# Loading the last 128 rows of w4 apart, onto the DMA engines with the lowest numbers

## Chip, cores and metric

One core of one Trainium2 chip. The metric is device time in microseconds (us) of one execution, median of several; lower is better. The span in a profile runs from the first to the last instruction and is some 1.8 us shorter than the device time.

## The reference, cut to what matters

```python
xn = _layernorm(A_x)                               # (4, 1, 576)
out = x + A(xn, k_cache, v_cache, wq, wo) + B(xn, w1, w2, w3, w4)
# A: one query per batch, 32 heads on 16 K/V heads, the last 2048 keys, times wo
# B: x1 = xn + hs (with one position the shifted branch is zero)
h2 = _gelu(_layernorm(x1) @ w3) @ w4               # w4: (4608, 576)
```

Nearly all of the work is reading: 16 K and 16 V tiles of 2 MB, wq, wo, w3, and w4 last.

## The kernel before

All loads but the 4.5 KB of x go from SyncE in one order: K and V by heads, wo by quarters, w3 after the third V, w4 at the very end, in six pieces. w4 is seen as 36 slots of 128 rows; slot u is one product per half of the output.

```python
W4_PIECES = [0, NFH, NF - 12, NF - 6, NF - 2, NF - 1, NF]      # NF = 36, NFH = 18

def load_w4():
    t = wp.tile([P, NF, D], BF16, tag="w", name="w4_sb")
    for lo, hi in zip(W4_PIECES, W4_PIECES[1:]):
        e = lo // NFH
        src = B_w4[e * (F // 2):(e + 1) * (F // 2), :].rearrange("(p i) n -> p i n", i=NFH)
        nc.sync.dma_start(out=t[:, lo:hi, :], in_=src[:, lo - e * NFH:hi - e * NFH, :])
# ... the end of the kernel:
    o_pick(hl)
    o_proj(hl)
    for lo, hi in pieces:
        mlp_out(lo, hi)          # gT[:, u, :] times w4[:, u, :], u from lo to hi
    # cast to bf16 on VectorE and ScalarE, one output DMA from SyncE
```

## Time and profile before

| | before |
|---|---|
| device time | 211.46 us (211.37 to 211.50, 3 runs) |
| span of the profiled run | 209.7 us |
| DMA: bytes, time of the load queue's packets | 87.17 MB, 97.5% of 16 engines |
| TensorE / VectorE busy | 69% / 54% |
| last landing; output DMA issued | 206.70; 207.59 us |

The kernel is bound by its loads: the engines of the DMA are full until 204.5 us, and what follows the last landing is 0.34 us of products, 0.45 of cast and the output DMA. The lines that carry this stand in the prediction. One reading is not a view of the page: the trace has, for every load, the time at which each DMA engine adds its 1 to the load's semaphore. I call the distance of an increment from the last one of that load its *lead*. For the last w4 piece of the kernel before:

```
leads, us: 1.75 1.63 1.60 1.56 1.54 1.35 1.28 1.13 0.85 | 0.20 0.14 0.13 0.08 0.07 0.06 0
```

Nine engines were early and seven late, although all had the same bytes.

### The profile page before, as it was taken

How to read it: one execution, taken by the hardware profiler on the slowest of the kernel's cores; microseconds unless marked ns; L12 is line 12 of the kernel's file. 1: busy time of each engine (PE TensorE's matmuls, PEld its weight loads, DVE VectorE, ACT ScalarE, POOL GpSimd, SP SyncE). 2: the span in 40 equal slices, each digit the busy share in tenths (PEclk: the TensorE clock that was granted, in tenths of full speed). 3: DMA queues.
4: the chain of work that ended last, by engine and by line, in shares of the span. 5: the costliest groups of instructions: out<-in, count | busy, mean ns of one | idle time of the engine just before them, and what ended most of it. 6: DMA issues, size and time to landing. Idle time of an engine off the chain costs nothing.

```text
span 209.7 us, 2335 instructions
## 1 busy us (share of the span) xinstructions
PE 144.6 (69%) x955; PEld 57.5 (27%) x955; DVE 114.1 (54%) x165; ACT 34.0 (16%) x64; POOL 8.7 (4%) x31
## 2 busy tenths in 40 slices
PE   0358297699690039555999997589794846897694
PEld 0123032233130013222443332134231312342362
DVE  3611877885910083926519879166849391764200
ACT  7512201021120001111122211111111201113100
POOL 4610000000000000000002000000000000000000
PEclk9999579999888558999999999889999997999669
DMA  7999999999999999999999999999999999999992
GB/s 295 406 406 441 428 428 419 444 427 428 434 443 416 431 434 415 444 425 441 422 428 431 437 411 439 431 434 431 427 428 434 419 443 428 425 437 448 407 405 80
DMA packets 6650, 87.31 MB, mean 416 GB/s; under 512 B 744, under 2 KB 1008, under 8 KB 1648
## 3 DMA queue, kind: packets, MB, share of 16 engines
q1 hardware_dynamic: 6632, 87.17, 97.5%
q8 instruction: 7, 0.11, 0.2%
q14 instruction: 3, 0.02, 0.0%
q10 hardware_dynamic: 8, 0.00, 0.0%
HBM read 87.17 MB, written 0.00 MB: 416 GB/s over the span
## 4 chain that ended last, share of the span: by engine, by line
DMA 75%; PE 12%; DVE 10%; ACT 1%; issue 0%; SPq 0%; DVEq 0%; ACTq 0%
DMA kn<-in_A_k_cache_dram 30%; DMA vn<-in_A_v_cache_dram 24%; DMA w_sb<-in_B_w_dram 15%; DVE kt L222 7%; DMA wq_sb<-in_A_wq_dram 6%; PE S L335 3%; PE g_ps L452 2%; PE q_ps L279 2%; PE acc L181 1%; PE O L387 1%; DVE qz L311 1%; PE gT_ps L464 1%; DVE mx L341 1%; PE oT L400 1%; ACT q_sb L290 1%; PE S L357 0%
## 5 line engine op out<-in xcount | busy, mean ns | idle before, releaser
L335 PE MATMUL S<-kt,qz 128*128 128x512 bf16 x256 | 73.4, 413 | 34.0 <-DVE kt L222 33.8
L222 DVE STREAM_TRANSPOSE kt<-kn 128x2048 int32<-128x2048 int32 x32 | 73.4, 2297 | 28.3 <-DMA kn<-in_A_k_cache_dram 26.8
L335 PEld LDWEIGHTS <-qz 128*128 128x128 bf16 x256 | 23.4, 105 | 64.2 <-issue 46.2
L387 PE MATMUL O<-vn,PT 128*32 128x512 bf16 x256 | 22.6, 394 | 12.2 <-DMA vn<-in_A_v_cache_dram 12.2
L363 ACT ACTIVATE E<-S 128x512 bf16<-128x512 f32 x16 | 9.5, 597 | 96.6 <-PE S L357 96.6
L369 DVE STREAM_TRANSPOSE PT<-E 128x512 bf16<-128x512 bf16 x16 | 11.4, 710 | 13.8 <-ACT E L363 13.8
L394 ACT ACTIVATE O_sb<-O,rd 128x512 f32<-128x512 f32 x16 | 11.0, 686 | 37.0 <-PE O L387 37.0
L387 PEld LDWEIGHTS <-PT 128*32 128x32 bf16 x256 | 5.9, 94 | 32.6 <-issue 32.3
L410 DVE TENSOR_REDUCE on<-oT 128x8 bf16<-128x128 f32 x16 | 4.6, 287 | 18.7 <-PE oT L400 18.7
L400 PE MATMUL oT<-ident_w,O_sb 128*128 128x128 f32 x64 | 11.9, 314 | 0.2 <-ACT O_sb L394 0.2
L341 DVE TENSOR_REDUCE mx<-S 128x1 f32<-128x512 f32 x16 | 10.5, 658 | 1.2 <-PE S L335 1.1
L400 PEld LDWEIGHTS oT<-ident_w,O_sb 128*128 128x128 f32 x64 | 7.5, 153 | 4.4 <-issue 3.4
L357 PE MATMUL S<-nm,j_row 8*128 8x512 bf16 x16 | 6.5, 408 | 2.1 <-DVE nm L353 1.9
L373 PE MATMUL dn<-rs,same_j 128*128 128x1 f32 x32 | 6.2, 264 | 0.4 <-DVE g_x L470 0.4
L373 PEld LDWEIGHTS dn<-rs,same_j 128*128 128x128 f32 x32 | 5.0, 195 | 4.5 <-issue 3.8
L181 PE MATMUL acc<-wo_sb,op 128*4 128x288 bf16 x64 | 5.5, 324 | 1.0 <-DVE op L432 1.0
L323 PE MATMUL S<-negbig,ohT 4*128 4x512 bf16 x16 | 6.2, 385 | 0.0
L181 PE MATMUL acc<-w_sb,gT 128*4 128x288 bf16 x72 | 5.7, 315 | 0.4 <-DMA w_sb<-in_B_w_dram 0.4
L279 PE MATMUL q_ps<-wq_sb,xnT 128*32 128x512 bf16 x40 | 4.4, 625 | 2.2 <-DMA wq_sb<-in_A_wq_dram 2.2
L452 PE MATMUL g_ps<-w_sb,ln2T 128*32 128x512 bf16 (+1 forms) x50 | 4.9, 443 | 0.0
L602 DVE CAST fin<-acc 4x288 bf16<-4x288 f32 x1 | 0.4, 447 | 8.0 <-PE acc L181 8.0
L474 POOL TENSOR_TENSOR g_u<-g_x 128x144 f32<-128x144 f32 x1 | 0.4, 426 | 101.4 <-DVE g_x L470 101.4
(86 smaller groups left out, 74.4 us busy)
## 6 DMA issues: line engine op xcount, KB each, us to landing
kn<-in_A_k_cache_dram SPq DMA_DIRECT2D x16, 2048.0 KB, 24.5
vn<-in_A_v_cache_dram SPq DMA_DIRECT2D x16, 2048.0 KB, 26.5
wo_sb<-in_A_wo_dram SPq DMA_DIRECT2D x4, 1152.0 KB, 27.1
w_sb<-in_B_w_dram SPq DMA_DIRECT2D x1, 4608.0 KB, 33.2
wq_sb<-in_A_wq_dram SPq DMA_DIRECT2D x1, 4096.0 KB, 12.8
w_sb<-in_B_w_dram SPq DMA_DIRECT2D x1, 2592.0 KB, 33.1
w_sb<-in_B_w_dram SPq DMA_DIRECT2D x2, 864.0 KB, 34.5
w_sb<-in_B_w_dram SPq DMA_DIRECT2D x2, 576.0 KB, 32.5
```

Source lines behind the costliest of these rows:

```text
L181: nc.tensor.matmul(out=acc_of(i), lhsT=lhsT, rhs=rhs[:, i * CW:(i + 1) * CW], start=False, stop=False, skip_group_check=True)
L222: nc.vector.transpose(out=kt[:], in_=src)
L279: nc.tensor.matmul(out=q_ps[r][g * QD:(g + 1) * QD, :], lhsT=xnT[:, k, :], rhs=wq_sb[:, col:col + NW], start=(j == 0), stop=False, skip_gr ...
L335: nc.tensor.matmul(out=S_ps[h][:], lhsT=qz[:, z0:z0 + P], rhs=kt[:, ib, c0:c0 + SC, e:2 * QD:2].rearrange("p c k -> p (c k)"), start=False ...
L341: nc.vector.reduce_max(out=mx[:], in_=S_ps[h][:], axis=AX.X)
L363: nc.scalar.activation(out=E[h][:].rearrange("p c k -> p (c k)"), in_=S_ps.pop(h)[:], func=ACT.Exp, scale=scale, accum_out=rs[:])
L369: nc.vector.transpose(out=PT[h][:], in_=E.pop(h)[:])
L373: nc.tensor.matmul(out=dn[:], lhsT=same_j[:], rhs=st.pop(("rs", h))[:], start=True, stop=True)
L387: nc.tensor.matmul(out=O_ps[h][g * QD:(g + 1) * QD], lhsT=PT[h][:, c, :], rhs=vn[:, :, c, :], start=(s == 0), stop=False, skip_group_check ...
L394: nc.scalar.activation(out=O_sb[h][:], in_=O_ps.pop(h)[:], func=ACT.Copy, scale=st.pop(("rd", h))[:, 0:1])
L400: nc.tensor.transpose(out=oT[:, s, :], in_=o[:, s, :], identity=ident_w[:, s * NJ:s * NJ + P])
L452: nc.tensor.matmul(out=g_ps[g * QD:(g + 1) * QD], lhsT=ln2T[:, k, :], rhs=rhs, start=(j == 0), stop=False, skip_group_check=True)
```

## The change

Its intent: give 128 rows (one of the 36 slots) to engines that are early. A load over 20 partitions in five groups runs on five engines, one over 12 in three groups on three, a single partition on one (that these are the lowest-numbered engines rests on the page that the prediction cites). So the 128 rows become ten narrow slots of 4, 12 or 20 rows, loaded among the last V loads into a K/V buffer, and the gelu result is turned so that it fits them. By rows of 1152 bytes: engine 0 gets 40, engines 1 and 2 get 24, engines 3 and 4 get 20, and every engine loses 8.

```diff
-    W4_PIECES = [0, NFH, NF - 12, NF - 6, NF - 2, NF - 1, NF]
+    NFM = NF - 1
+    W4_PIECES = [0, NFH, NFM - 11, NFM - 6, NFM - 2, NFM - 1, NFM]
+    X0 = F - P
+    XB, XC, XA = 0, 4, 5            # slots of 4, 12 and 20 rows; XS = 10, NX = 20
+    def x4_rows(part):
+        t = w_tiles["x4"]           # one K/V buffer, taken after V 13
+        if part == "A":
+            src = B_w4[X0 + 28:F, :].rearrange("(q g i) n -> g q (i n)", q=4, g=5)
+            nc.sync.dma_start(out=t[0:NX, XA * D:XS * D], in_=src)
+        elif part == "C":
+            src = B_w4[X0 + 16:X0 + 28, :].rearrange("(q g) n -> g q n", q=4)
+            nc.sync.dma_start(out=t[0:12, XC * D:XA * D], in_=src)
+        else:
+            q, lo, hi = part
+            src = B_w4[X0 + 4 * q + lo:X0 + 4 * q + hi, :].rearrange("(q i) n -> q (i n)", q=1)
+            nc.sync.dma_start(out=t[q:q + 1, (XB + lo) * D:(XB + hi) * D], in_=src)
+    X_AFTER = {13: ["A", (0, 0, 4)], 14: [(1, 0, 4), (2, 0, 2), "C"], 15: [(2, 2, 4), (3, 0, 2), (3, 2, 4)]}
 # cut: 15 more up-projection products, 10 transposes and two copies that make gT's ten narrow slots
+    def mlp_extra(lo, hi):
+        acc_matmuls([(gT[0:k, NFM + s, :], t[0:k, s * D:(s + 1) * D])
+                     for s in range(lo, hi) for k in (4 if s < XC else 12 if s == XC else NX,)])
     o_scale(hl - 1)
+    mlp_extra(XC, XS)
     for s in range(NSL):
         pv(hl, s)
     ...
     o_pick(hl)
+    mlp_extra(XB, XC)
     o_proj(hl)
```

More of the change, by code (lines that the diff above doesn't have):

```diff
@@ L132, in load_w3, with x_cols, load_x4 @@
         w_tiles["w3"] = t
-    W4_PIECES = [0, NFH, NF - 12, NF - 6, NF - 2, NF - 1, NF]
+    NFM = NF - 1
+    W4_PIECES = [0, NFH, NFM - 11, NFM - 6, NFM - 2, NFM - 1, NFM]
+    X0 = F - P
+    XB, XC, XA = 0, 4, 5
+    XS = 10
+    NX = 20
+    NS = NFM + XS
+    def x_cols(ap):
+        b, c, a = ap[:, 0:16], ap[:, 16:28], ap[:, 28:P]
+        return [(0, b.rearrange("p (q i) -> p i q", q=4)), (16, c.rearrange("p (q g) -> p g q", q=4)),
+                (28, a.rearrange("p (q g i) -> p i g q", q=4, g=5))]
     def load_w4():
-        t = wp.tile([P, NF, D], BF16, tag="w", name="w4_sb")
+        t = wp.tile([P, NFM, D], BF16, tag="w", name="w4_sb")
         for lo, hi in zip(W4_PIECES, W4_PIECES[1:]):
             e = lo // NFH
-            src = B_w4[e * (F // 2):(e + 1) * (F // 2), :].rearrange("(p i) n -> p i n", i=NFH)
+            n = NFH - e
+            src = B_w4[e * (F // 2):e * (F // 2) + P * n, :].rearrange("(p i) n -> p i n", i=n)
             nc.sync.dma_start(out=t[:, lo:hi, :], in_=src[:, lo - e * NFH:hi - e * NFH, :])
         w_tiles["w4"] = t
+    def load_x4():
+        t = kvp.tile([P, NC, Dh], BF16, tag="kv", name="x4")
+        w_tiles["x4"] = t[:].rearrange("p c d -> p (c d)")
+    def x4_rows(part):
[11 more added lines that the diff above has]
+    X_AFTER = {13: ["A", (0, 0, 4)], 14: [(1, 0, 4), (2, 0, 2), "C"], 15: [(2, 2, 4), (3, 0, 2), (3, 2, 4)]}
     ident_bf = const.tile([P, P], BF16)
@@ L166 @@
     qz = cleared([P, ZP + Hkv * 4 * P], "qz")
-    gT = const.tile([P, NF, B], BF16, name="gT")
+    gT = const.tile([P, NS, B], BF16, name="gT")
     op = const.tile([P, WOR, B], BF16, name="op")
@@ L439 @@
     G_CHUNKS = [(e, 4 * g, 4) for e in range(2) for g in range(NQD)] + [(e, 16, 2) for e in range(2)]
-    xs = const.tile([P, NF, B], F32, name="g_x")
+    xs = const.tile([P, NS, B], F32, name="g_x")
+    nc.gpsimd.memset(xs[:, NFM:, :], 0.0)
     g_sb = {}
@@ L450, in mlp_g @@
                 base, k = (j * F + e * (F // 2), j) if j < KJ else (KJ * F, KJ + e)
-                rhs = w3[:, base:base + F // 2].rearrange("p (q i) -> p q i", i=NFH)[:, :, i0:i0 + n]
-                nc.tensor.matmul(out=g_ps[g * QD:(g + 1) * QD], lhsT=ln2T[:, k, :], rhs=rhs,
-                                 start=(j == 0), stop=False, skip_group_check=True)
+                m = P * (NFH - e)
+                cols = w3[:, base:base + m].rearrange("p (q i) -> p q i", q=P)
+                row = g_ps[g * QD:(g + 1) * QD]
+                mms = [(row[:, :, 0:min(n, NFH - e - i0)], cols[:, :, i0:min(i0 + n, NFH - e)])]
+                if e and r == 2:
+                    for lo, rhs in x_cols(w3[:, base + m:base + F // 2]):
+                        sizes = rhs.shape[1:]
+                        hi = lo + sizes[0] * sizes[1] * (sizes[2] if len(sizes) > 2 else 1)
+                        names = "x y z"[:2 * len(sizes) - 1]
+                        kw = dict(zip(names.split()[1:], sizes[1:]))
+                        mms.append((row[:, lo:hi, 1].rearrange(f"p ({names}) -> p {names}", **kw), rhs))
+                for out, rhs in mms:
+                    nc.tensor.matmul(out=out, lhsT=ln2T[:, k, :], rhs=rhs,
+                                     start=(j == 0), stop=False, skip_group_check=True)
         m = len(chunks) * QD
@@ L460, in mlp_turn @@
         n, m = chunks[0][2], len(chunks)
-        gT_ps = ps_m.tile([P, n, m, QD], F32, tag="m", name="gT_ps")
+        xn = XS if r == 2 else 0
+        gT_all = ps_m.tile([P, n * m + xn, QD], F32, tag="m", name="gT_ps")
+        gT_ps = gT_all[:, 0:n * m].rearrange("p (u g) x -> p u g x", u=n)
         gs = g_sb.pop(r)
@@ L468, in mlp_turn @@
         else:
-            dst = xs[:].rearrange("p (e i) b -> p i e b", e=2)[:, 16:18]
+            e1 = slice(QD, 2 * QD)
+            for s in range(XS):
+                off = 4 * s if s < XC else 16 if s == XC else 28 + NX * (s - XA)
+                nc.tensor.transpose(out=gT_all[0:NX, n * m + s, :], in_=gs[e1, off:off + NX, 1],
+                                    identity=ident_f[e1, e1])
+            nc.vector.tensor_copy(out=xs[0:NX, NFM:, :], in_=gT_all[0:NX, n * m:, 0:B])
+            nc.vector.tensor_copy(out=xs[:, NFM - 1, :], in_=gT_ps[:, 0, 1, 0:B])
+            dst = xs[:, 16:18, :].unsqueeze(2)
+            gT_ps = gT_ps[:, :, 0:1]
         nc.vector.tensor_copy(out=dst, in_=gT_ps[:, :, :, 0:B])
     def mlp_act():
-        u = const.tile([P, NF, B], F32, name="g_u")
+        u = const.tile([P, NS, B], F32, name="g_u")
         nc.gpsimd.tensor_tensor(out=u[:], in0=xs[:], in1=xs[:], op=ALU.mult)
@@ L479, in mlp_act @@
         nc.gpsimd.tensor_tensor(out=gT[:], in0=u[:], in1=xs[:], op=ALU.mult)
+    def mlp_extra(lo, hi):
+        t = w_tiles["x4"]
+        acc_matmuls([(gT[0:k, NFM + s, :], t[0:k, s * D:(s + 1) * D])
+                     for s in range(lo, hi) for k in (4 if s < XC else 12 if s == XC else NX,)])
     def mlp_out(lo, hi):
@@ L490 @@
             order.append(("K", h + 3))
+        if h == min(X_AFTER):
+            order.append(("X", h))
     W3_AFTER = ("V", 2)
@@ L498, in flush_loads @@
                 load_wo(h // WOQ)
-            load_kv(kind, h)
+            if kind == "X":
+                load_x4()
+            else:
+                load_kv(kind, h)
+            if kind == "X" or kind == "V" and h > min(X_AFTER):
+                for part in X_AFTER.get(h, []):
+                    x4_rows(part)
             pos["n"] += 1
```

## The prediction

> **What bounds the kernel now.** I read the page first: queues, then the chain that ended last.
>
> ```profile
> DMA  7999999999999999999999999999999999999992
> ...
> q1 hardware_dynamic: 6632, 87.17, 97.5%
> q8 instruction: 7, 0.11, 0.2%
> ...
> DMA 75%; PE 12%; DVE 10%; ACT 1%; issue 0%; SPq 0%; DVEq 0%; ACTq 0%
> ```
>
> One queue of loads fills the 16 DMA engines from 2 us to the last slice. 87.17 MB pass in about 204 us, and DMA carries 75% of the chain. Time can be won only in how soon the last load lands, so I read the end, first as a timeline:
>
> ```profile
> 197.79 0.37 PE L419 MATMUL R<-on,sel_wo 128*128 128x32 bf16 x8 [0.38 <-DVE on L410]
> ...
> 199.14 2.08 PE L181 MATMUL acc<-wo_sb,op 128*4 128x288 bf16 x16 [0.97 <-DVE op L432]
> ...
> 201.01 4.65 PE L181 MATMUL acc<-w_sb,gT 128*4 128x288 bf16 x60
> 206.03 1.01 PE L181 MATMUL acc<-w_sb,gT 128*4 128x288 bf16 x12 [0.36 <-DMA w_sb<-in_B_w_dram]
> ...
> 207.06 0.45 DVE L602 CAST fin<-acc 4x288 bf16<-4x288 f32 x1 [7.98 <-PE acc L181]
> ```
>
> PE does 60 products on w4 without a gap, waits 0.36 us for the piece of four slots, and does the last 12. The landing records of the trace give 205.98, 206.33 and 206.70 us for the last three pieces. The last product starts near 206.75 and takes 0.29, so the end (207.04) is the last landing plus 0.34. Next, windows over the last microseconds (the last two columns are the DMA engines' busy share and GB/s):
>
> ```profile
> 202.00:204.50 2.50, 2.50 (x38) 1.69 (x36) 0.00 (x0) 0.00 (x0) 0.00 (x0) 0.87 0.99 406
> 204.50:205.00 0.50, 0.50 (x12) 0.35 (x8) 0.00 (x0) 0.00 (x0) 0.00 (x0) 1.00 0.90 348
> 205.00:205.50 0.50, 0.50 (x12) 0.35 (x7) 0.00 (x0) 0.00 (x0) 0.00 (x0) 1.00 0.57 224
> 205.50:206.00 0.50, 0.16 (x4) 0.00 (x0) 0.00 (x0) 0.00 (x0) 0.00 (x0) 1.00 0.45 159
> 206.00:206.50 0.50, 0.47 (x8) 0.35 (x9) 0.00 (x0) 0.00 (x0) 0.00 (x0) 1.00 0.24 85
> ```
>
> The share falls from 0.99 to 0.57 and 0.45 before the end: about half of the engines have run dry while the rest still work. All got the same bytes, so they were delayed unequally. The 16 landing increments of the last piece say by how much: ahead of the last one by 1.75, 1.63, 1.60, 1.56, 1.54, 1.35, 1.28, 1.13, 0.85 us, and then seven within 0.20. Their mean lead is 0.91 us: perfect balance could win that and no more.
>
> The seven late ones have a cause that I can date. The instruction queue moved seven 16 KB packets, at 30.8, 64.7, 103.2, 121.3, 147.2, 178.9 and 198.4 us, each 0.9 us long. After each of them one more of the 16 increments of every load is late: 1 of 16 for the load that lands at 32.85, 4 at 125.6, 7 at the end. The landings before the first packet lie within 0.5 us.
>
> **What the Trainium skill says.** "DMA: Bandwidth & Descriptors", section "Why a DMA increments its semaphore by 16 and not by 1": a load issued from SyncE runs on the largest number of engines up to 16 that divides the slowest dimension of both sides, and on the lowest-numbered ones. The 20 partitions by 5 groups of this change thus go to engines 0 to 4, the 12 by 3 to 0 to 2, a single row to engine 0. The trace before cannot confirm it: its weight loads all have 128 partitions, and packets carry no engine number. The same page, "Queues, rings and completion order": each engine drains its own ring in order. The trace agrees: an engine late at 32.85 stays late, and no later load repairs it. "Runtime: NRT & Kernel Launch", "Instruction fetch mechanics": instructions come in 16 KiB blocks of 256, at a cost called "mostly hidden". The blocks agree: TensorE and weight-load records pass 182, 464, 719, 972, 1240, 1480 and 1752 at the seven packets, 262 apart on average. The cost does not: the increments show some 1.4 us lost on the engine concerned.
>
> **The change, part by part.** It takes 128 of the 4608 rows of w4 (147 KB, 8 rows of 1152 bytes from each engine) out of the wide loads and gives them to the engines that it takes to be early.
>
> 1. Every engine loses one slot of the piece of six: 6912-byte packets of 262 ns become 5760. From 262 against 178 ns for 4608 bytes, 1152 bytes cost 42 ns, so 8 x 42 = 0.34 us. For the seven late engines, if they are not among engines 0 to 4, that is all: 206.70 becomes 206.36.
> 2. Load A gives engines 0 to 4 four packets of 5760 bytes, 220 ns each: 0.88 us. C gives engines 0 to 2 four of 1152 (51 ns, some 4 of it overlapped): 0.19. The six single-row loads give engine 0 two packets of 4608 (178) and four of 2304 (estimate 93): 0.73. Semaphore packets of 9 ns add up to 0.07. Net: engine 0 +1.53 us, engines 1 and 2 +0.75, engines 3 and 4 +0.55.
> 3. If engine 0 is the earliest (204.96), it ends at 206.49 and engines 1 to 4 at about 205.9: the last landing moves from 206.70 to 206.49, 0.21 us earlier. If it is only the fifth earliest (205.16), it ends at 206.69 and nothing is won.
> 4. TensorE: ten slots of two products added and one slot taken away, 18 net. Twelve stand before the last head's value products, where PE sat idle 1.61 us for the value load (192.81 to 194.41); at the 50 to 85 ns spacing seen at full and half clock they take at most 1.0. Eight stand in the 0.97 us idle before the output projection: at half clock 0.7. Both fit. The first w4 stretch becomes 58 products, so PE keeps its slack of about 0.4 us. The two narrow groups come from 15 extra up-projection products and 10 transposes near 107 us; the queue then holds some 18 us of issued loads (a V issued at 119.89 lands at 142.87), so a few microseconds there are covered.
> 5. Issue: the x4 tile takes one of the six K/V buffers, so the last V waits for one buffer more. The waits of the DMA queue show a further limit:
>
> ```profile
> SPq L141 <- DMA vn<-in_A_v_cache_dram: 9.0, 2, 4.5
> ...
> SPq L141 <- DMA kn<-in_A_k_cache_dram: 4.5, 1, 4.5
> ```
>
> The w4 pieces wait for loads issued eight earlier: eight completion semaphores go round. Eight narrow loads use them up. The last V then goes out when the last K lands (179.7, before: 166.8), and the first w4 piece when the next to last V lands (189.4, before: 167.4). The earliest engine finishes the last V at 192.5; an issue needs 1.1 us to its first packet (0.74 to 1.87 at the start). Some 1.9 us remain, so no engine runs dry.
>
> Sum: -0.21 us of 211.46, 211.25.
>
> **Rivals.** *Engine 0 to 4 are not the early ones.* Nothing in the profile names an engine; only the shape of the change (most for engine 0, least for 3 and 4, nothing for 5 to 15) says that its author saw room there. If a late engine is 3 or 4, the end moves by +0.55; if it is 0, by +1.53 to 213.0. *An eighth instruction block.* About 43 more products and transposes, with their weight loads, make 1932 records about 2018. Block eight would fall near record 2010, in the last products. If its packet hits an engine that still has work, 0.9 to 1.4 us come back; on an idle one it costs nothing. Against it: the early engines are by then nearly done. *Thinner prefetch starves the DMA engines* (step 5, should issue or generation be slower than I took): each gap adds its length, perhaps 1 to 3 us. For it: in-flight bytes before w4 drop to about one V load. Against it: even that is 4.9 us of work per engine. *PE takes over the end*: if the eight late extras ran over the gap by more than 0.4 us, the gain would be gone; a higher granted clock in the busier stretch would help instead. It was 0.50 from 198 to 202 and binds nothing today.
>
> **Range and chances.** The gain cannot pass 0.34 us plus noise (the three runs span 0.13), so the low end is 210.9. Aim correct but engine 0 not quite the earliest leaves 0 to 0.2. One bad hit of the first two rivals adds 0.5 to 1.5, and I give them together one chance in four, so the high end is 212.0. Over 2% either way would need 4.2 us: faster is ruled out by the 0.91 us of imbalance, slower asks for repeated starvation. Chances: faster 0.01, same 0.97, slower 0.02.
>
> **What would show it.** Right: the last piece lands near 206.5, its 16 increments lie within about 1 us instead of 1.75, the busy share of the last windows stays higher, and the chain still ends in a w4 piece and its products. Step 2 is checked by the increments of A, C and the single rows: 5, 3 and 1 of them late, the others at issue. Step 4 is wrong if PE waits for nothing before the last pieces; step 5 if the DMA share dips near 189 to 193. The prediction is wrong if one increment of the last piece stands alone after the others by over 0.5 us (engine 0 overloaded, or a block landed on it), or if an eighth packet on the instruction queue comes before 206 us.

## The result, and the profile after

211.42 us (211.33 to 211.51, 6 runs) against 211.45 (211.29 to 211.53, 6 runs) of the kernel before in the same rounds: ratio 0.9999, 95% interval 0.9987 to 1.0012. Nothing clear of noise. From the page of the changed kernel, its queues and the chain that ended last:

```profile
DMA  7999999999999999999999999999999999999992
...
q1 hardware_dynamic: 6684, 87.17, 97.6%
q8 instruction: 8, 0.13, 0.2%
...
DMA 66%; DVE 15%; PE 13%; issue 2%; ACT 1%; SPq 1%; POOL 1%; DVEq 0%; POOLq 0%; ACTq 0%
```

The bytes are the same, and there is an eighth instruction packet. The timeline of its end:

```profile
192.74 0.90 PE L212 MATMUL acc<-x,gT 12*4 12x288 bf16 x12
...
198.56 1.12 PE L212 MATMUL acc<-x,gT 4*4 4x288 bf16 x8
...
201.48 4.07 PE L212 MATMUL acc<-w_sb,gT 128*4 128x288 bf16 x58
205.94 1.04 PE L212 MATMUL acc<-w_sb,gT 128*4 128x288 bf16 x12 [0.39 <-DMA w_sb<-in_B_w_dram]
...
207.02 0.45 DVE L670 CAST fin<-acc 4x288 bf16<-4x288 f32 x1 [7.47 <-PE acc L212]
```

The added products (first two lines) stand where they were meant to; PE still waits for the piece of four slots (0.39 us, before 0.36), and the cast begins at 207.02, before at 207.06. Windows over the last microseconds (DMA share and GB/s in the last two columns):

```profile
204.50:205.00 0.50, 0.50 (x12) 0.34 (x8) 0.00 (x0) 0.00 (x0) 0.00 (x0) 1.00 0.89 337
205.00:205.50 0.50, 0.50 (x10) 0.26 (x5) 0.00 (x0) 0.00 (x0) 0.00 (x0) 1.00 0.72 265
205.50:206.00 0.50, 0.11 (x4) 0.06 (x3) 0.00 (x0) 0.00 (x0) 0.00 (x0) 1.00 0.49 171
206.00:206.50 0.50, 0.50 (x10) 0.39 (x10) 0.00 (x0) 0.00 (x0) 0.00 (x0) 1.00 0.09 30
```

From 205.0 to 205.5 the share rose from 0.57 to 0.72, and from 206.0 to 206.5 it fell from 0.24 to 0.09: the load is better spread, and after 206 hardly a packet is under way. Yet the last landing is 206.66, where it was 206.70. The leads say why:

```
leads, us: 2.03 2.00 1.89 1.72 1.02 | 0.61 0.59 0.55 0.54 0.53 0.50 0.46 0.44 0.30 | 0.06 0
```

The late group has moved to 206.04 to 206.36 (before, it ended at 206.70), the gain that was meant; two engines now end alone after it, at 206.59 and 206.66.

**Which two.** The increments of the narrow loads name their engines. The load A has five increments beside one that comes soon after the issue, long before the data (0.4 to 1.3 us in these loads); C has three, a single row one. Taking off A's own work (four packets of 220 ns and a semaphore packet, 0.89 us) gives the leads of engines 0 to 4 over the last engine at the 14th V load, which A follows in the queue: 1.82, 1.80, 1.57, 1.28 and 0.59. The single row behind A lands 0.20 after 183.84, so engine 0 is the one with 1.57. The load C (engines 0 to 2) has no increment that continues the 0.59, so that is engine 3 or 4. The net costs of the prediction, 1.53 for engine 0 and 0.55 for engines 3 and 4, leave 1.57 - 1.53 = 0.04 and 0.59 - 0.55 = 0.04 us: two engines whose lead was all spent. Which of the two lone increments, 206.59 or 206.66, is engine 0's, the trace doesn't say.

### The profile page after: what moved, and what is told of

Same layout as the page of the kernel before. It is cut to its first block, busy times and chain, and to the rows that moved or that the text cites. A ratio compares the mean times of both kernels' runs of the same rounds, so it can differ in the third digit from the quotient of the medians.

```text
span 209.6 us, 2422 instructions
## 1 busy us (share of the span) xinstructions
PE 149.7 (71%) x984; PEld 60.1 (29%) x998; DVE 114.4 (55%) x167; ACT 34.1 (16%) x64; POOL 9.0 (4%) x32
## 4 chain that ended last, share of the span: by engine, by line
DMA 66%; DVE 15%; PE 13%; issue 2%; ACT 1%; SPq 1%; POOL 1%; DVEq 0%; POOLq 0%; ACTq 0%
DMA kn<-in_A_k_cache_dram 42%; DVE kt L253 12%; DMA vn<-in_A_v_cache_dram 10%; DMA w_sb<-in_B_w_dram 7%; DMA wq_sb<-in_A_wq_dram 6%; PE S L366 4%; PE g_ps L495 3%; PE q_ps L310 2%; PE oT L431 1%; PE O L418 1%; PE acc L212 1%; DVE PT L400 1%; DVE mx L372 1%; PE S L388 1%; DVE qz L342 1%
## 5 line engine op out<-in xcount | busy, mean ns | idle before, releaser
L366 PEld LDWEIGHTS <-qz 128*128 128x128 bf16 x256 | 23.9, 107 | 62.9 <-issue 45.8
L418 PE MATMUL O<-vn,PT 128*32 128x512 bf16 x256 | 23.4, 406 | 8.0 <-DMA vn<-in_A_v_cache_dram 8.0
L431 PE MATMUL oT<-ident_w,O_sb 128*128 128x128 f32 x64 | 12.6, 333 | 0.3 <-ACT O_sb L425 0.3
L431 PEld LDWEIGHTS oT<-ident_w,O_sb 128*128 128x128 f32 x64 | 8.2, 164 | 5.3 <-issue 4.3
L495 PE MATMUL g_ps<-w_sb,ln2T 128*32 128x512 bf16 (+5 forms) x65 | 6.2, 406 | 0.0
L212 PE MATMUL acc<-w_sb,gT 128*4 128x288 bf16 x70 | 5.1, 298 | 0.4 <-DMA w_sb<-in_B_w_dram 0.4
L523 DVE COPY g_x<-gT_ps 128x64 f32<-128x64 f32 (+1 forms) x3 | 0.6, 198 | 8.2 <-PE gT_ps L509 8.2
L527 POOL TENSOR_TENSOR g_u<-g_x 128x180 f32<-128x180 f32 x1 | 0.5, 487 | 103.1 <-DVE g_x L523 103.1
```

The lines of the kernel that those rows point to most:

```text
L212: nc.tensor.matmul(out=acc_of(i), lhsT=lhsT, rhs=rhs[:, i * CW:(i + 1) * CW], start=False, stop=False, skip_group_check=True)
L366: nc.tensor.matmul(out=S_ps[h][:], lhsT=qz[:, z0:z0 + P], rhs=kt[:, ib, c0:c0 + SC, e:2 * QD:2].rearrange("p c k -> p (c k)"), start=False ...
L418: nc.tensor.matmul(out=O_ps[h][g * QD:(g + 1) * QD], lhsT=PT[h][:, c, :], rhs=vn[:, :, c, :], start=(s == 0), stop=False, skip_group_check ...
L431: nc.tensor.transpose(out=oT[:, s, :], in_=o[:, s, :], identity=ident_w[:, s * NJ:s * NJ + P])
L495: nc.tensor.matmul(out=out, lhsT=ln2T[:, k, :], rhs=rhs, start=(j == 0), stop=False, skip_group_check=True)
```

## The experiments

The theory (**overloaded engines**) is that engine 0 and one of engines 3 and 4 were given more work than they had lead, and end the kernel. The rivals: TensorE's longer tail or an eighth instruction block sets the end; the narrow loads, or the shorter issue-ahead, cost something as such. For comparing landings between traces I use a shift: the landing of the last piece minus that of the 14th V load, minus the 22.18 us (206.70 - 184.52) of the kernel before. It takes out where a trace began. It is no finer than some 0.14 us: in e7, which moves no byte between engines, it is +0.14.

| run | what | device time, us | before, same rounds | ratio (95%) | shift |
|---|---|---|---|---|---|
| changed kernel | | 211.42 | 211.45 | 0.9999 (0.9987 to 1.0012) | -0.04 |
| e1 | probes of 15 to 1 engines | 213.9 | 211.50 | one run | |
| e2 | no narrow loads | 211.15 | 211.50 | 0.9989 (0.9977 to 1.0002) | -0.33 |
| e3 | no single-row loads | 211.93 | 211.50 | 1.0027 (1.0013 to 1.0040) | -0.23 |
| e4 | no load over five engines | 211.25 | 211.50 | 0.9991 (0.9979 to 1.0004) | -0.32 |
| e5 | dealt out anew | 212.05 | 211.65 | 1.0026 (1.0011 to 1.0040) | +0.14 |
| e6 | the changed kernel again | 211.29 | 211.65 | 0.9992 (0.9979 to 1.0005) | -0.33 |
| e7 | before, two DMAs more | 211.75 | 211.65 | 1.0010 (0.9998 to 1.0022) | +0.14 |
| e8 | before, three DMAs more | 212.40 | 211.53 | 1.0039 (1.0026 to 1.0052) | 0.00 |
| e9 | before, 96 products more | 221.52 | 211.53 | 1.0471 (1.0447 to 1.0496) | 0.00 |
| e10 | dealt out anew, second try | 211.57 | 211.53 | 1.0007 (0.9994 to 1.0021) | +0.20 |

All results passed the comparison with the reference; e2, e3 and e4 read wrong rows on purpose, and the rows concerned are too few for the tolerance.

**e1, the probes.** Tiny loads of k partitions, k from 15 down to 1, behind the last three V loads.

```diff
+    PROBE = {13: (15, 14, 13, 12, 11), 14: (10, 9, 8, 7, 6), 15: (5, 4, 3, 2, 1)}   # after V h
+    def probe(ks):
+        for k in ks:
+            nc.sync.dma_start(out=probe_t.pop()[0:k, :], in_=B_w4[0:k, 0:32])
```

> The kernel before, with 18 tiny loads (64 bytes a row) of 15, 14, ... 1 partitions behind the last three V loads and of 12, 8 and 4 behind the last w4 piece; each runs on as many engines as it has partitions, lowest-numbered first, so the landing that k has and k-1 has not is engine k-1's. Theory (overloaded engines): engines 0, 1, 2 and one of 3 and 4 show a lead of 1.2 to 1.8 us over the last engine at the last V loads, the other one of 3 and 4 a lead of 0.5 to 1.1 (hit by an 8 KB instruction packet); some of engines 5 to 15 lead by 1.5 us too. Rival (engines 0 to 4 are not the early ones): at least one of them lies in the late group, within 0.25 us of the last. Time: before plus 0 to 0.8 us (the tiny packets), not read.

Each load had k increments and the early one, so k engines it was. Landings of some of them, in us:

```
k=12: 183.47 183.52 183.53 183.63 183.71 183.74 183.75 | 184.26 184.56 | 185.12 185.15 185.20
k=11: 183.64 183.69 183.71 183.83 183.91 183.92 183.96 | 184.44 184.74 | 185.29 185.39
k=10: 187.92 187.93 187.96 188.15 188.15 188.19 188.29 | 188.72 189.02 | 189.72
k=6:  188.63 188.69 188.96                             | 189.44 189.76 | 190.61
```

All sixteen had eight early engines behind the first of these V loads, k = 15 has seven; each further step down to k = 10 takes a late one away. If a load takes the lowest-numbered engines first, engine 15 is early and engines 10 to 14 are late. From k = 10 to 6 only early ones go: engines 6 to 9 are early. Engines 0 to 5 hold both middle ones and one late one; the late one is gone at k = 5 and is engine 5. So the aim was right as to the late group: none of engines 0 to 4 is in it, and going on to a sixth engine would have met it. But both middle ones are among the five, where I had expected one (leads of 0.98 and 0.69 at the first of these V loads). My estimate of the time missed: 2.4 us over before, not 0 to 0.8. In this trace one engine of 4 to 7 ended 1.2 us after all others; engine 5, late already, is the one that fits if the instruction packet at 199.3 hit it, so it seems that an engine can be hit twice.

**e2, e3, e4, loads left out.** The products stay and read the last wo tile.

```diff
+    LEFT_OUT = "ABC"      # e2; "B" (the single rows) in e3; "A" (the load over five engines) in e4
     def x4_rows(part):
+        if (part if isinstance(part, str) else "B") in LEFT_OUT:
+            return
```

> The changed kernel without its eight narrow loads; the 20 products on them read the last wo tile instead (wrong result on purpose), at the same places. Theory (engine 0 and one of engines 3 and 4 were given more than their lead): the last landing moves to about 206.36, 0.3 us before that of either kernel; time 211.1, ratio to before 0.9985. Rivals (TensorE's longer tail sets the end, or the eighth instruction block does): both are still there, so time 211.4, ratio 1.000. Rival (shorter issue-ahead cost something at the end): the issue order is that of before again, so the whole bulk of the increments would move, not just the last two.

> Only the six single-row loads of engine 0 are left out (wrong result on purpose). Theory: engine 0 gets 0.8 us back and leaves the end, but the other overloaded engine (3 or 4, hit by an 8 KB packet before) still lands last, at 206.6 to 206.7: time 211.4, ratio to before 1.000. If engine 0 alone were the culprit: last landing 206.36, time 211.1, ratio 0.9985.

> Only the load over five engines is left out (wrong result on purpose). Theory: both overloaded engines get 0.88 us back, engine 0 ends near 205.7 and the other near 205.8; the late group ends the kernel at 206.36: time 211.1, ratio to before 0.9985. If the load over five engines were not to blame: last landing still 206.66, ratio 1.000.

e2 and e4 came out as the theory says: shifts of -0.33 and -0.32 us, the medians 0.35 and 0.25 us lower (their intervals still touch 1). The tail's products and the eighth packet (at 204.4) are all in e2, so they don't set the end. The times alone would not carry this: the changed kernel itself, run again as e6, has a ratio of 0.9992, between theirs and 1 but within their noise. The evidence is in the landings. Windows of e2:

```profile
204.50:205.00 0.50, 0.50 (x10) 0.26 (x5) 0.00 (x0) 0.00 (x0) 0.00 (x0) 1.00 0.55 217
205.00:205.50 0.50, 0.04 (x2) 0.00 (x0) 0.00 (x0) 0.00 (x0) 0.00 (x0) 1.00 0.48 177
205.50:206.00 0.50, 0.35 (x6) 0.26 (x7) 0.00 (x0) 0.00 (x0) 0.00 (x0) 1.00 0.38 134
206.00:206.50 0.50, 0.50 (x10) 0.25 (x4) 0.00 (x0) 0.00 (x0) 0.00 (x0) 1.00 0.00 0
```

No packet is left for the DMA engines after 206.0 (the last increment comes at 206.33), and PE is nearly idle from 205.0 to 205.5: it waits. In e3 the loads did end earlier than I had said (shift -0.23, not 0): engine 3 or 4 had a lead of 0.79 in that trace and kept 0.79 - 0.55 = 0.24 of it, so relieving engine 0 was enough there. But the time went up by 0.4 us. Its timeline has the reason behind the loads:

```profile
206.76 0.45 DVE L676 CAST fin<-acc 4x288 bf16<-4x288 f32 x1 [7.03 <-PE acc L216]
206.79 0.40 ACT L678 ACTIVATE fin<-acc 4x288 bf16<-4x288 f32 x1 [9.71 <-PE acc L216]
207.70 0.30 SPq L679 DMA_DIRECT2D out_dram<-fin  x1
```

The casts end at 207.21, and the output DMA is issued at 207.70; in the kernel before it follows the cast after 0.08 us. Nothing that the profile shows lies between. e7 and e8 take that up.

**e5, a correct version with the rows dealt out by leads.**

```diff
+    XG = {"D": (1, 4, 1), "B": (4, 2, 2), "C": (4, 3, 4), "A": (4, 5, 3)}   # rows per engine and slot, engines, slots
```

> A correct version: the same 128 rows on engines 0 to 4, dealt out by the leads that the traces gave (about 1.6, 1.7, 1.2, 0.6 and 1.7 us for engines 0 to 4): 60 rows over five engines in 3 slots, 48 over three in 4, 16 over two in 2, 4 over four in 1, so 37, 37, 29, 13 and 12 rows in place of 40, 24, 24, 20 and 20; four loads in place of eight. Theory (overloaded engines): engine 0 +1.37, engine 2 +1.0, engine 3 +0.26 us, so the last landing comes at 206.45 to 206.5, 0.2 us before that of either kernel; time 211.25 where before is 211.5, ratio 0.999. Rivals (TensorE's tail, or the narrow loads as such): ratio 1.000, last landing 206.6 to 206.7.

Slower, by 0.26%. My assignment was wrong: the load over engines 0 and 1 lands at 189.20 and 189.73, so one of these two was the middle one, with a lead of 1.19 by A's increments, and 37 rows (net +1.37) make 0.18 us too much; the shift is +0.14. One engine ends 0.47 us after all others. The profiled execution (211.77) was the fastest of the six, which went up to 212.66; what made the others slower, no trace shows.

**e6, the changed kernel again, on that chip.** No edit.

> The changed kernel unaltered, as a control on this chip. Theory: last landing 206.55 to 206.7, closing with one or two single engines (0, and 3 or 4) 0.2 us or more after the others; ratio to before 1.000. If its ratio is below 0.999 the effect seen in the runs without narrow loads isn't theirs.

Here the leads of engines 0 to 4 were 1.90, 1.88, 1.87, 1.07 and 0.88 (engine 0 has one of the first three), so engine 0 keeps 0.34 and engine 3 or 4 keeps 0.33 (the 1.07 is engine 1 or 2, as C continues it, and keeps 0.32): enough for nearly the whole gain of 0.34, and the shift is -0.33. By the shift, the same program won all or nothing of it in two profiled executions. Part of that is the yardstick: the engine that ended the 14th V load stood 0.28 us behind the next one in e6 and 0.15 in the changed kernel's first trace, and leads and shift count from it. As they stand, the last landings are 206.52 here, 206.66 there and 206.70 before. Of what I expected, the two lone engines were not there, and the ratio was lower, though its interval holds 1.

**e7 and e8, the stop in front of the output DMA.** The kernel before with its first w4 piece cut into three or four.

```diff
-    W4_PIECES = [0, NFH, NF - 12, ...]
+    W4_PIECES = [0, 6, 12, NFH, NF - 12, ...]        # e7: two DMA instructions more
+    W4_PIECES = [0, 5, 10, 14, NFH, NF - 12, ...]    # e8: three more
```

> The kernel before, with the first w4 piece (18 slots) issued as three of 6: the same bytes, no narrow load, two more DMA instructions on SyncE, as many as the run without single-row loads (3) had. That run ended its products 0.3 us early and yet took 0.4 us more than before: SyncE stood 0.46 us between the end of the casts and the output DMA. Theory (SyncE fetches its next instruction block there, and two more instructions bring the boundary to that place): last landing 206.7 as before, the same gap of 0.4 to 0.5 us in front of the output DMA, time 211.9 to 212.1, ratio 1.002 to 1.003. Rival (the narrow loads, or the order of the completion semaphores, made that gap): no gap, ratio 1.000.

> The kernel before with its first w4 piece issued as four pieces: three more DMA instructions on SyncE, the same bytes. In the traces SyncE stands still once near its end for 0.44 to 0.48 us: between its second and third closing wait in the kernel before, right behind the output DMA with two more instructions (the split in three), in front of the output DMA in the run without single-row loads. Theory (an instruction block ends there and the next one isn't there yet): with three more instructions the stop falls in front of the output DMA again; last landing as before (206.7 to 207.0), 0.4 to 0.5 us between the end of the casts and the output DMA, time 0.4 to 0.6 us over before, ratio 1.002 to 1.003. Rival (it came with the narrow loads): no such stop, ratio 1.000 to 1.001.

e7 missed: the gap was not in front of the output DMA but right behind it (0.45 us, 208.23 to 208.68), where it costs nothing, as the output is still under way. In the kernel before it is two instructions further on (208.09 to 208.54, between two closing waits). Two instructions more had moved it by two. So three more should put it in front of the output DMA, and e8 shows that:

```profile
207.06 0.45 DVE L602 CAST fin<-acc 4x288 bf16<-4x288 f32 x1 [7.44 <-PE acc L181]
207.09 0.40 ACT L604 ACTIVATE fin<-acc 4x288 bf16<-4x288 f32 x1 [10.08 <-PE acc L181]
208.00 0.34 SPq L605 DMA_DIRECT2D out_dram<-fin  x1
```

Same last landing (206.69), same cast, output DMA 0.41 us later than before; 0.74 us of span and 0.87 of time in all. I had said 0.4 to 0.6: the rest is that the output's own wait now comes first among five closing waits instead of last, some 0.22 us, and that the output took 1.39 us to land instead of 1.29. The narrow loads are not needed for it.

The other traces say more. Counted in the trace, waits included, the stop stands in front of the 80th record of SyncE in all twelve of them, 0.44 to 0.46 us long. In the changed kernel that is between its first two w4 issues, as its chain shows, with loads enough in the queue:

```profile
189.69 0.36 SPq L153
190.04 0.45 issue
190.49 0.36 SPq L153
```

After each stop an 8 KB instruction packet starts, 0.62 to 0.87 us later where the loads are over (208.65 in e8) and 3.1 to 4.0 us later where they are not (194.51 in the changed kernel). So the stop is at a boundary in SyncE's instructions. What SyncE waits for there no record names: the packet shown begins after the stop.

**e9, more instruction blocks.** In the heads 4 to 15 the small product of the row sums is done nine times instead of once.

```diff
-        nc.tensor.matmul(out=dn[:], lhsT=same_j[:], rhs=st.pop(("rs", h))[:], start=True, stop=True)
+        rs = st.pop(("rs", h))
+        for _ in range(9 if 4 <= h else 1):
+            nc.tensor.matmul(out=dn[:], lhsT=same_j[:], rhs=rs[:], start=True, stop=True)
```

> The kernel before with eight repeats of the small product of the row sums in each of the heads 4 to 15 (96 products and 96 weight loads more, same result): TensorE then needs its eighth instruction block about 110 records before its end, near 195 us. Theory (each 16 KB block delays one engine by 1.4 us, always another one): eight packets of 16 KB before 200 us, eight instead of seven increments of the last w4 piece within 0.4 us of the last, last landing 206.6 to 206.9, time as before (ratio 0.999 to 1.002). If blocks fall on engines at random, one increment may stand alone 1.2 to 1.4 us after the others: time up to 212.9. If the blocks aren't the cause of the late group: still seven.

The time missed by 10 us: the repeats (each is two products and two weight loads in the trace, so 192 more of each and not 96) made PE the bound, and it ended its products 10 us after the last landing. The question was for the loads, and those answer it. The queues of e9, the ninth packet being at 213.8, after all loads:

```profile
q1 hardware_dynamic: 6632, 87.17, 93.1%
q8 instruction: 9, 0.15, 0.3%
```

Eight packets before 199 us, and eight increments of the last piece within 0.21 us (0.21, 0.20, 0.19, 0.13, 0.07, 0.04, 0.02, 0) where before there were seven. One more block, one more late engine: with the dates of the seven in the prediction, the blocks make the late group.

**e10, the second try at dealing out:** 37, 29, 29, 17 and 16 rows.

> A correct version again, now with engine 1 as the one with a short lead (the first attempt gave 37 rows to engine 1, whose lead was 1.2 us): 80 rows over five engines in 4 slots, 36 over three in 3, 8 single-engine rows in 2, 4 over four in 1, so 37, 29, 29, 17 and 16 rows. Theory: engine 0 +1.39, engines 1 and 2 +0.99, engine 3 +0.44 us against leads of 1.6, 1.2, 1.7 and 0.6 to 0.8; last landing 206.4 to 206.55, time 0.15 to 0.3 us under before, ratio 0.9985 to 0.9995. If leads wander from run to run by more than they differ here: one or two single increments 0.2 to 0.5 us after the others, ratio 1.000.

The leads were 1.58, 1.41, 1.21, 0.84 and 0.74 this time, and the 0.74 belonged to engine 1 or 2, where 29 rows cost +0.99: 0.25 too much (C continues 0.74 or 0.84, and 0.74 fits better). The single rows behind C make engine 0 the one with 1.21, against +1.39: 0.18 too much. Two engines end alone, at 206.69 and 206.73; the shift is +0.20. No dealing out that I could find suits all traces: the smaller two of the five leads were 1.28/0.59, 1.15/0.79, 1.19/0.74, 1.07/0.88 and 0.84/0.74 in the five traces that have the load A.

One sum runs through all of these: the shift should be the largest of (net cost - lead) over the receiving engines, and no lower than the -0.34 of the lost slot. It gives -0.04 for the changed kernel, -0.34, -0.24 and -0.34 for e2, e3 and e4, +0.18 for e5, -0.32 for e6 and +0.25 for e10; measured are -0.04, -0.33, -0.23, -0.32, +0.14, -0.33 and +0.20. That is what shows the theory.

## Why the prediction was right, point by point

It said -0.21 us inside a range of 210.9 to 212.0, and "same"; measured is -0.03, and -0.36 by the medians of the repeat (e6), neither clear of noise. "Same" was safe, as at most 0.34 us could be won; that the profiled run won nothing has a cause which step 3 had wrong. Of the signs named in advance, the last landing near 206.5 came at 206.66, and two of them failed: the 16 increments spread over 2.03 us and not 1, since early engines outside 0 to 4 (6 to 9 and 15 in e1) were given nothing; and the eighth packet, named as a sign of being wrong, did come before 206 us, without harm.

- **Bound, late group, instruction packets:** right. e9 adds a packet and an engine is added to the late group; e1 shows its engines apart from 0 to 4.
- **Mean lead:** the 16 leads shown average 0.84 us, not the 0.91 that the prediction says; nothing rests on the difference.
- **"Mostly hidden":** "Runtime: NRT & Kernel Launch", "Instruction fetch mechanics", speaks of what crossing a block boundary costs the engine that runs the instructions. The 1.4 us are lost by a DMA engine, so the two don't contradict each other.
- **Step 1** (the late group ends at 206.36): measured 206.36.
- **Step 2** (net +1.53 for engine 0, +0.55 for 3 and 4): the two ended at 206.59 and 206.66, so 0.11 and 0.04 before 206.70. From leads of 1.57 and 0.59 that is +1.46 and +0.55, or the other way round +1.53 and +0.48. The sizes hold.
- **Step 3** is the one that failed, in the words "engines 1 to 4 at about 205.9": I compared engine 0 alone with the leads, and gave 3 and 4 a place among the early ones. One of them is a middle engine in every trace that can tell, with 0.59 to 0.88 us of lead against +0.55. Before, the middle leads of 1.13 and 0.85 could be seen; I didn't ask whose they were. The condition in the same step ("if it is only the fifth earliest, it ends at 206.69 and nothing is won") did come true for engine 0 in the profiled run, with a lead of 1.57 where the fifth earliest has 1.54. The rival "engines 0 to 4 are not the early ones" was thus half right: not late, but not all early.
- **Step 4:** the twelve products took 0.90 us in the idle time, as said; the eight took 1.12 instead of 0.7 and still fitted. The output projection moved from 199.14 to 199.61, but not by them: it begins 0.06 to 0.07 us after VectorE's last reduction in both kernels. That chain was late by 0.47 from the spreading products on (198.26, before 197.79): 0.26 from the V load, which landed later, and 0.20 from value products that took longer, with a granted clock of 0.84 from 194 to 196 us (before 0.96). PE's slack of 0.39 us held.
- **Step 5:** the last V was issued at 179.71 and the first w4 piece at 189.69 (said: 179.7 and 189.4), and the DMA share from 188 to 194 stayed at 1.01 to 1.05. Nothing starved.
- **The eighth block** came at 204.8 us, on an engine that had finished: no lead changes between the pieces before and after it.

What stays open: which instructions the 8 KB packets at 47 and 149 us carry (in all twelve traces they come after the same numbers of records of SyncE, 22 and 60 or 61, but ScalarE's, 21 and 63 or 64, fit as well), and why the leads of the engines they hit wander from trace to trace; and whether a fixed deal can win anything over many executions. None of the versions here beats both kernels beyond noise.

## What to carry to other kernels

When the loads bound a kernel, look at when each DMA engine ends, not only at the mean share: the last engine sets the time, and instruction blocks make engines unequal. Before moving bytes from late engines to early ones, find out which engine has which lead (a load of k partitions, then of k-1, tells them apart), and check each receiving engine's lead against its new work, in more than one trace: 0.34 us were to be won here, and two engines out of five gave it back. A few DMA instructions more on SyncE can cost 0.9 us, without a byte more to load, by where an instruction boundary falls near the output (e8).

## What the Trainium skill lacked or had wrong

- "Runtime: NRT & Kernel Launch", "Instruction fetch mechanics", calls the cost of crossing a 16 KiB boundary "mostly hidden" and says nothing of what the fetch costs other loads. Here each block delayed one DMA engine by some 1.4 us, for good: seven packets, seven late engines of sixteen; eight in e9. With the loads bounding the kernel that is up to 0.84 us of its time (the mean lead).
- None of the pages that I read has this: SyncE stood still for 0.44 to 0.46 us in front of its 80th record in all twelve traces; in front of the output DMA (e3, e8) that made the kernel slower (e8: ratio 1.0039).
- Nor this: beside the packets of 16 KB the traces show two 8 KB packets, at 47 and 149 us (309 ns each), with some 0.75 us of delay for the engine concerned, and a third that follows SyncE's stop (194.51 us in the changed kernel, 209.19 before).
- "DMA: Bandwidth & Descriptors" has no figure for tiny loads queued behind each other on one engine: in e1 loads of 64 bytes a row (packets of 11 ns) landed some 0.17 to 0.20 us apart on the same engine. What the page says of the number of engines of a load, the increments confirm: 5, 3 and 1 for the narrow loads, and every k from 15 to 1.
